# Cosine through an integer conversion read from PSUM, and float64 weights converted 1024 wide

## The chip, the cores and the metric

The kernel runs on one core of a Trainium2 chip. The metric is the device time of one execution in microseconds (us). Each kernel is run several times, and the median counts.

## The reference

Three layers follow one another on 4608 tokens (8 batches of 576) of 512 values:

```python
kv = np.einsum('bhsd,bhse->bhde', k, v)                  # attention without softmax, 8 heads of 64
out = np.einsum('bhsd,bhde->bhse', q, kv)
x = out / np.sqrt(np.mean(out * out, -1, keepdims=True) + 1e-6) * g_norm
h = x @ w_in                                             # 512 -> 2048, w_in and w_out are float64
g = h * np.cos(h)
x = g @ w_out                                            # 2048 -> 512
idx = np.argmax(x @ w_gate, axis=1)                      # one of 8 experts for each token
out[mask] = gate_w[mask, None] * (np.maximum(xe @ w1[e], 0.0) @ w2[e])   # expert e on its tokens
```

The change is in the middle layer: in how `h * cos(h)` is computed, and in how `w_in` and `w_out` are brought from float64 to pairs of float16.

## The kernel before

Every float32 operand is split into two float16 parts, high and low, and a product is three matmuls (high·high, high·low, low·high). TensorE issues them through `mm3`, lines 102 to 104; the profile tells the products apart by their tiles. A split elsewhere is `split` (lines 88 and 89): ScalarE writes the high part, VectorE the low one.

The program is one straight list, written out by hand (`manual_schedule`): each engine works through its own queue in order, and waits where a semaphore is not yet there. Nothing is reordered.

Before the loop stands a prelude (`SEQ0`) with the attention of the first batch and the first two weight tiles of `w_in`. Then come nine blocks of 512 tokens, `b` = 0 to 8, each of 32 half-steps `hs`; `fb = hs // 2` counts the 16 slices of 128 of the 2048 hidden columns. An even half-step issues `g1(b, fb)`: 12 matmuls into the PSUM tile `hps`. An odd one issues `g2(b, fb - 2)`: 12 matmuls that take `gh`, `gl` of the slice two before and the weights `woh`, `wol` into the four tiles `yps`. The last two `g2` of a block are issued at the start of the next. The PSUM tiles `hps` come from a pool of two (`psh`), the tiles `yps` from a pool of four.

Between `g1` and `g2` of a slice lies the cosine. `h` arrives in turns (the weights are scaled by 1 / 2 pi on the way, and by 2 pi in `w_out`). ScalarE copies `hps` to `hs` in SBUF (line 475). VectorE adds a large number so that the sum rounds to whole turns (line 482) and takes it off again, and `hs` as well (line 483); ScalarE takes the absolute value (478) and the sine (479). In `cos_b`, VectorE multiplies by `hs` (496), ScalarE writes `gh` (493), and GpSimd writes `gl` (494).

In block 0 the weights are converted as well, in `conv_w`, a tile of 1 MB in two halves of 512 columns a partition: three VectorE instructions put the float32 bits together (228, 231, 234), ScalarE scales (240) and writes the high half (241), and GpSimd subtracts for the low half (242). One half falls on each half-step up to `hs` = 25, and on 28 and 29; the instructions of ScalarE and GpSimd for a half are issued one half-step later. The tiles come through a ring of four staging tiles; the next load is issued when a tile has been read (`used`).

The rest is side work, put into half-steps by the tables `SEQ1` and `SEQ`: attention of the next block (query splits `nat`, `kvh`/`kvl`, products `ops`, the squares `sq` on GpSimd, their sums `ssq`, the Newton steps of `norm`, lines 422 to 434, the products with `rs` on GpSimd, line 443, then the splits `nat` and the DMA transposes into `xT`, of which `c3` is the last), and the routing of the block before (`r_evac`: four splits from `yps` to `yrow`, at half-step 3). In the last block, `split_x` converts weights of the first expert (`w1h`, `w1l`) ahead of the copy of `hps`, and at half-step 22 `pass_head` casts the counts on VectorE (line 586) and has TensorE add them up (`tps`, line 588). After the blocks come the eight experts, without cosine or conversion.

Of the kernel before, what the change touches and what calls it, by code (L numbers as in the profile page):

```python
# [18 lines left out]
# Float32 operands are split into float16 pairs (hi + lo, scaled by powers of  # L19
# two so that both parts are normal numbers); a product is hi*hi + hi*lo + lo*hi.  # L20
# [5 lines left out]
# Each expert's list has room for all tokens; its first CAP rows are computed  # L26
# for every expert, what lies beyond them only if it is there. The last block
# of tokens goes behind row HEAD, so that the rows before are complete early.
# [7 lines left out]
def tile_attn_moe_moe(ctx: ExitStack, tc: tile.TileContext, q, k, v, g_norm, w_in, w_out, w_gate, w1, w2, out):  # L36
# [17 lines left out]

    const = ctx.enter_context(tc.tile_pool(name="const", bufs=1))
# [7 lines left out]
    # a row: the token (hi, lo), its logits and its number  # L63
# [28 lines left out]
    # Steps of the side work are emitted in two parts, the second (returned) a  # L92
    # little later, so that no engine waits for another's part of the same step.
# [12 lines left out]
    def setup_consts(pre):  # L106
# [10 lines left out]
        # summed over the partitions: the row where the list of each expert starts  # L117
# [13 lines left out]
    # ------------------------------------------------------------------  # L131
    # Phase 1: attention and the dense layer, block by block of 512 tokens
    # ------------------------------------------------------------------
# [3 lines left out]
    gring = ctx.enter_context(tc.tile_pool(name="gring", bufs=LAG + 2))  # L137
    p1 = ExitStack()
# [29 lines left out]
    def load_kv_first():  # L168
        # in parts, in the order of use
        for i in range(2):  # L170
            for nm in "kv":
                load_kv_part(0, nm, 4 * i, 4 * i + 4)
            if i == 0:
                for nm in "kv":
                    load_kv_left(0, nm)
# [20 lines left out]
    # The weights of the dense layer come in float64: its bits are cut to float32 on the chip.  # L196
# [12 lines left out]
    def conv_w(kind, c, i):  # L209
        t = wst[kind, c]  # L210
        if kind == "i":
            src = t[:, :, 128 * i:128 * i + 128]
            o = (c % 4) * 256 + 128 * i
            dh, dl = [w[c // 4].rearrange("p (k f) -> p k f", k=KD)[:, :, o:o + 128] for w in (wih, wil)]
            sc = gs
        else:
            src = t[:, i:i + 1]
            o = (c % 4) * 2 + i
            dh, dl = [w[c // 4].rearrange("p (k f) -> p k f", k=8)[:, o:o + 1] for w in (woh, wol)]
            sc = S_WOUT * TWO_PI  # L220
        sh = list(src.shape)[:3]
        lo, hi = src[:, :, :, 0], src[:, :, :, 1]
        vi = b3.tile(sh, I32, tag="vi", name="vi")
        vf = vi.bitcast(F32)

        def bits(n):
            if n == 0:
                nc.vector.tensor_scalar(out=vi, in0=hi, scalar1=3, scalar2=0x3FFFFFFF, op0=ALU.logical_shift_left,
                                        op1=ALU.bitwise_and)
            elif n == 1:  # L230
                nc.vector.scalar_tensor_tensor(out=vi, in0=hi, scalar=-0x40000000, in1=vi, op0=ALU.bitwise_and,
                                               op1=ALU.bitwise_or)
            else:
                nc.vector.scalar_tensor_tensor(out=vi, in0=lo, scalar=29, in1=vi, op0=ALU.logical_shift_right,
                                               op1=ALU.bitwise_or)
                if i == 1:
                    used()

        def late():
            nc.scalar.activation(out=vf, in_=vf, func=AF.Copy, scale=sc)  # L240
            nc.scalar.activation(out=dh, in_=vf, func=AF.Copy)
            nc.gpsimd.tensor_tensor(out=dl, in0=vf, in1=dh, op=ALU.subtract)  # L242

        return [call(bits, n) for n in range(3)], late

    # Loads run ahead as far as the ring of staging tiles allows.
# [20 lines left out]
    def split_kv(b, nm, j):  # L267
        # a quarter of the tokens (j < 4), or those left over
# [41 lines left out]
    # The first two batches: VectorE is taken by the weights, so k and v go in  # L310
    # as they are; only k is laid out anew.
# [11 lines left out]
    def hot(n):  # L323
        # keeps TensorE at its full clock until the data is there
        ps = psh.tile([128, 512], F32, tag="h", name="hot")
        for _ in range(n):
            nc.tensor.matmul(out=ps[:, 0:128], lhsT=ident, rhs=ident, start=True, stop=True)
# [30 lines left out]
    def split_t(dst, src, scale):  # L358
        # split and turned
# [58 lines left out]
    def norm(b, i):  # L418
        # rs = (mean square + eps) ** -0.5: a bit-level guess and Newton steps
# [47 lines left out]
    # h is kept in turns (h / 2 pi, scaled): cos sees the distance from the nearest whole turn  # L467
    def cos_a(b, fb, ps):
        big = 1.5 * 2.0 ** 23 * S_H
        hs = b3.tile([128, 512], F32, name="hs")  # L470
        u = b3.tile([128, 512], F32, name="u")
        hu[b, fb] = (hs, u)

        def first():
            nc.scalar.activation(out=hs, in_=ps, func=AF.Copy, scale=S_H / (S_X * S_WIN))  # L475

        def late():
            nc.scalar.activation(out=u, in_=u, func=AF.Abs, scale=TWO_PI / S_H)  # L478
            nc.scalar.activation(out=u, in_=u, func=AF.Sin, scale=-1.0, bias=half_pi)  # L479

        return first, [
            lambda: nc.vector.tensor_scalar(out=u, in0=hs, scalar1=big, scalar2=None, op0=ALU.add),  # L482
            lambda: nc.vector.scalar_tensor_tensor(out=u, in0=u, scalar=big, in1=hs, op0=ALU.subtract, op1=ALU.subtract)  # L483
        ], late

    def cos_b(b, fb):
        hs, u = hu.pop((b, fb))
# [8 lines left out]
        return [lambda: nc.vector.tensor_tensor(out=u, in0=hs, in1=u, op=ALU.mult)], late  # L496
# [43 lines left out]
    def choose(b):  # L540
        # first index of the largest logit, and how many earlier tokens chose each expert
# [41 lines left out]
    def totals():  # L583
        # over all partitions: where each expert's next row is
# [37 lines left out]
    # ------------------------------------------------------------------  # L622
    # Phase 2: one expert after the other
    # ------------------------------------------------------------------
# [87 lines left out]
    # ------------------------------------------------------------------  # L712
    # Program
    # ------------------------------------------------------------------
# [7 lines left out]
    # the order in which the staging tiles are used  # L722
# [12 lines left out]
    for e in range(E):  # L735
        for c in range(2):
            add_load(load_w1, e, c, ready=lambda e=e: e == 0 or xs_done)
        for c in range(2):
            add_load(load_w2, e, c, ready=lambda e=e: e == 0 or xs_done)

    # The side work: what comes before the first block, and in which of a block's 32
    # steps the parts for the next block (the second one, those after) are emitted.
    ATT = {"a": attn_a, "b": attn_b, "d": attn_d, "n": attn_n, "m": attn_m, "c": attn_c}
    SEQ0 = ("hot a0 kc0 a1 kv0 kc1 a2 a3 kv1 wi00 b0 b1 d0 d1 b2 b3 kd0 d2 d3 kd1 kd2 kd3 kw0 n0 Wi00 "
            "n1 m0 m1 m2 m3 wi01 c0 c1 c2 c3 Wi01 wi10 wi11 Wi10 Wi11").split()
# [5 lines left out]
    with tc.manual_schedule():  # L751
        pump()
        nc.gpsimd.memset(half_pi, math.pi / 2.0)
# [235 lines left out]
```

## Time and profile before

| | |
|---|---|
| time, median of 3 runs | 1341.68 us (1340.82 to 1343.31) |
| span of the profiled execution | 1342.1 us |
| TensorE busy | 1269.9 us, 95% |
| VectorE busy | 771.8 us, 58% |
| ScalarE busy | 664.8 us, 50% |
| GpSimd busy | 398.4 us, 30% |

A busy TensorE means that a matmul is under way; one matmul is recorded longer (0.38 us for 512 columns) than the distance to the next. The page cuts the span into 40 slices of 33.6 us. In its row for TensorE the first six slices read 6, 8, 7, 7, 6, 8 (tenths), and nearly all later ones 9; in the row for VectorE the second to the fifth read 9. The row of the clock granted to TensorE reads 7 to 9 in the first seven slices and 9 (which stands for 90% and more) after that. So the time in which TensorE is not at work lies in the prelude and block 0, with some in the last block and at the end of the program.

### The profile page before, as it was taken

What the parts mean: (1) busy time and instruction counts of PE and PEld (TensorE: products, weight loads), DVE (VectorE), ACT (ScalarE), POOL (GpSimd) and SP (SyncE); (2) the same over time, 40 slices, a digit from 0 to 9 for tenths busy, and PEclk for the clock granted to TensorE, in tenths of its full rate; (3) what the DMA queues carried; (4) which work ended last, traced back from release to release, by engine and by line L of the source; (5) the groups of instructions that cost most, each with busy time, mean ns of one, the idle gap of its engine ahead of it and who ended that gap; (6) DMA issues with size and microseconds to landing.
All of it is one profiled execution on the core that took longest, in us unless ns stands there. A gap on an engine that the chain in (4) does not pass through costs nothing.

```text
span 1342.1 us, 18677 instructions
## 1 busy us (share of the span) xinstructions
PE 1269.9 (95%) x7236; PEld 661.1 (49%) x7236; DVE 771.8 (58%) x1323; ACT 664.8 (50%) x1178; POOL 398.4 (30%) x386
## 2 busy tenths in 40 slices
PE   6877689999999999999999999989999999999995
PEld 6423235445444554454444444435665665655553
DVE  4999965767767568577574565554543334235211
ACT  3565556565665656656655555444533333334221
POOL 3356622524425335244253352232100100110110
PEclk7889889999999999999999999999999999999998
DMA  8455369353513425144145330034935425525000
GB/s 264 160 134 180 94 177 281 93 115 62 149 42 73 133 56 133 42 64 96 24 64 166 86 73 16 17 108 121 273 116 155 127 90 170 141 95 115 32 21 23
DMA packets 242929, 146.97 MB, mean 110 GB/s; under 512 B 197262, under 2 KB 214670, under 8 KB 242832
## 3 DMA queue, kind: packets, MB, share of 16 engines
q1 hardware_dynamic: 236064, 126.51, 37.6%
q0 software_dynamic: 6080, 19.18, 4.0%
q8 instruction: 58, 0.95, 0.3%
q14 instruction: 39, 0.32, 0.1%
q10 hardware_dynamic: 688, 0.02, 0.0%
HBM read 78.99 MB, written 31.03 MB: 82 GB/s over the span
## 4 chain that ended last, share of the span: by engine, by line
PE 66%; DVE 17%; issue 6%; ACT 6%; DMA 3%; POOL 1%; SPq 0%; POOLq 0%; DVEq 0%; ACTq 0%
PE yps L102 6%; PE hps L102 6%; PE yps L104 6%; PE yps L103 6%; PE hps L103 6%; PE hps L104 6%; PE ops L102 5%; PE ops L104 5%; PE ops L103 5%; PE h1ps L102 4%; PE h1ps L103 4%; PE h1ps L104 4%; DVE u L482 3%; DVE u L483 3%; DVE u L496 2%
## 5 line engine op out<-in xcount | busy, mean ns | idle before, releaser
L494 POOL TENSOR_TENSOR gl<-u,gh 128x512 f16<-128x512 f32 x144 | 173.9, 1208 | 392.3 <-ACT gh L493 330.9
L102 PE MATMUL yps<-woh,gh 128*128 128x512 f16 x576 | 224.3, 389 | 21.0 <-ACT gh L493 14.9
L104 PE MATMUL yps<-woh,gl 128*128 128x512 f16 x576 | 225.5, 391 | 13.1 <-POOL gl L494 12.9
L103 PE MATMUL yps<-wol,gh 128*128 128x512 f16 x576 | 224.4, 390 | 1.6 <-POOL wol L242 1.6
L102 PE MATMUL hps<-xT,wih 128*128 128x512 f16 x576 | 219.0, 380 | 4.4 <-DMA xT<-nat 2.5
L103 PE MATMUL hps<-xT,wih 128*128 128x512 f16 x576 | 218.5, 379 | 0.3 <-DVE xT L89 0.3
L104 PE MATMUL hps<-xT,wil 128*128 128x512 f16 x576 | 218.3, 379 | 0.0
L478 ACT ACTIVATE u<-u 128x512 f32<-128x512 f32 x144 | 90.7, 630 | 252.1 <-DVE u L483 222.2
L482 DVE TENSOR_SCALAR u<-hs 128x512 f32<-128x512 f32 x144 | 120.1, 834 | 112.7 <-ACT hs L475 112.3
L496 DVE TENSOR_TENSOR u<-hs,u 128x512 f32<-128x512 f32 x144 | 102.9, 715 | 124.9 <-ACT u L479 124.8
L697 DVE SCALAR_TENSOR_TENSOR h1l<-h1ps,h1h 128x256 f16<-128x256 f32 (+1 forms) x128 | 62.7, 490 | 184.6 <-ACT h1h L696 180.4
L102 PE MATMUL h1ps<-xeT,w1h 128*128 128x256 f16 (+1 forms) x512 | 153.2, 299 | 0.6 <-DVE h1l L697 0.3
L104 PE MATMUL h1ps<-xeT,w1l 128*128 128x256 f16 (+1 forms) x512 | 153.2, 299 | 0.0
L103 PE MATMUL h1ps<-xeT,w1h 128*128 128x256 f16 (+1 forms) x512 | 153.2, 299 | 0.0
L709 POOL DMA_INDIRECT out_dram<-ob,ei x40 | 39.4, 986 | 356.0 <-ACT ob L708 296.8
L483 DVE SCALAR_TENSOR_TENSOR u<-u,hs 128x512 f32<-128x512 f32 x144 | 121.2, 841 | 5.0
L493 ACT ACTIVATE gh<-u 128x512 f16<-128x512 f32 x144 | 90.6, 629 | 64.1 <-DVE u L496 63.9
L104 PE MATMUL ops<-w2h,h1l 128*128 128x512 f16 x320 | 121.3, 379 | 0.0
L103 PE MATMUL ops<-w2l,h1h 128*128 128x512 f16 x320 | 121.3, 379 | 0.0
L102 PE MATMUL ops<-w2h,h1h 128*128 128x512 f16 x320 | 121.3, 379 | 0.0
L708 ACT ACTIVATE ob<-ops,gt 128x512 f32<-128x512 f32 x40 | 27.5, 688 | 176.8 <-PE ops L104 146.0
L479 ACT ACTIVATE u<-u,half_pi 128x512 f32<-128x512 f32 x144 | 103.9, 722 | 4.7
(154 smaller groups left out, 1892.2 us busy)
## 6 DMA issues: line engine op xcount, KB each, us to landing
w1s<-in_moe_w_dram SPq DMA_DIRECT2D x16, 1024.0 KB, 4.8
w2s<-in_moe_w_dram SPq DMA_DIRECT2D x16, 1024.0 KB, 5.5
xs<-pre SPq DMA_DIRECT2D x8, 1320.0 KB, 7.3
wst<-in_moe_w_in_dram SPq DMA_DIRECT2D x8, 1024.0 KB, 5.8
wst<-in_moe_w_out_dram SPq DMA_DIRECT2D x8, 1024.0 KB, 4.8
kst<-in_k_dram SPq DMA_DIRECT2D x7, 1024.0 KB, 8.7
vst<-in_v_dram SPq DMA_DIRECT2D x7, 1024.0 KB, 6.8
qst<-in_q_dram SPq DMA_DIRECT2D x28, 256.0 KB, 4.7
```

The costliest lines, as they stand in the source:

```text
L102: nc.tensor.matmul(out=o, lhsT=ah, rhs=bh, start=first, stop=False)
L103: nc.tensor.matmul(out=o, lhsT=ah, rhs=bl, start=False, stop=False)
L104: nc.tensor.matmul(out=o, lhsT=al, rhs=bh, start=False, stop=last)
L478: nc.scalar.activation(out=u, in_=u, func=AF.Abs, scale=TWO_PI / S_H)
L479: nc.scalar.activation(out=u, in_=u, func=AF.Sin, scale=-1.0, bias=half_pi)
L482: lambda: nc.vector.tensor_scalar(out=u, in0=hs, scalar1=big, scalar2=None, op0=ALU.add),
L483: lambda: nc.vector.scalar_tensor_tensor(out=u, in0=u, scalar=big, in1=hs, op0=ALU.subtract, op1=ALU.subtract)
L493: nc.scalar.activation(out=gh, in_=u, func=AF.Copy)
L494: nc.gpsimd.tensor_tensor(out=gl, in0=u, in1=gh, op=ALU.subtract)
L496: return [lambda: nc.vector.tensor_tensor(out=u, in0=hs, in1=u, op=ALU.mult)], late
L697: nc.vector.scalar_tensor_tensor(out=dl, in0=ps, scalar=0.0, in1=dh, op0=ALU.max, op1=ALU.subtract)
L709: nc.gpsimd.indirect_dma_start(out=out, out_offset=bass.IndirectOffsetOnAxis(ap=eid[e, i], axis=0), in_=ob, in_offset=None, bounds_check=N ...
```

## The change

Cosine: ScalarE writes `n`, an int32 tile, straight from `hps`, as h plus a quarter turn, rounded by the conversion. VectorE then computes h − n in one instruction that reads `hps` in PSUM. The range is moved by the quarter turn so that ScalarE's sine takes h − n with a positive scale and the bias, without an absolute value. The product with h reads `hps` a second time. So `hps` is held until `cos_b`, and `hs` is gone.

Weights: `conv_w` works on the whole tile, 1024 columns. It has three parts: `bits` (three VectorE instructions), `high` (one ScalarE instruction with the scale in it), `low` (one VectorE instruction in place of ScalarE's scaling and GpSimd's subtraction). They are issued at half-steps `hs`, `hs + 1` and `hs + 2`. The comments are taken out; line numbers shift.

```diff
-    def conv_w(kind, c, i):
-        t = wst[kind, c]
+    def conv_w(kind, c):
+        t = wst.pop((kind, c))
...
-        vi = b3.tile(sh, I32, tag="vi", name="vi")
+        vi = vip.tile(sh, I32, tag="vi", name="vi")
...
-        def late():
-            nc.scalar.activation(out=vf, in_=vf, func=AF.Copy, scale=sc)
-            nc.scalar.activation(out=dh, in_=vf, func=AF.Copy)
-            nc.gpsimd.tensor_tensor(out=dl, in0=vf, in1=dh, op=ALU.subtract)
+        def high():
+            nc.scalar.activation(out=dh, in_=vf, func=AF.Copy, scale=sc)
+
+        def low():
+            nc.vector.scalar_tensor_tensor(out=dl, in0=vf, scalar=sc, in1=dh, op0=ALU.mult, op1=ALU.subtract)
+
+        return [bits, high, low]
...
         def first():
-            nc.scalar.activation(out=hs, in_=ps, func=AF.Copy, scale=S_H / (S_X * S_WIN))
+            nc.scalar.activation(out=n, in_=ps, func=AF.Copy, scale=1.0 / (S_X * S_WIN), bias=0.25)
 
         def late():
-            nc.scalar.activation(out=u, in_=u, func=AF.Abs, scale=TWO_PI / S_H)
-            nc.scalar.activation(out=u, in_=u, func=AF.Sin, scale=-1.0, bias=half_pi)
+            nc.scalar.activation(out=u, in_=u, func=AF.Sin, scale=SIN_SCALE, bias=half_pi)
 
         return first, [
-            lambda: nc.vector.tensor_scalar(out=u, in0=hs, scalar1=big, scalar2=None, op0=ALU.add),
-            lambda: nc.vector.scalar_tensor_tensor(out=u, in0=u, scalar=big, in1=hs, op0=ALU.subtract, op1=ALU.subtract)
+            lambda: nc.vector.scalar_tensor_tensor(out=u, in0=ps, scalar=1.0 / (S_X * S_WIN), in1=n, op0=ALU.mult,
+                                                   op1=ALU.subtract)
         ], late
...
-        return [lambda: nc.vector.tensor_tensor(out=u, in0=hs, in1=u, op=ALU.mult)], late
+        return [lambda: nc.vector.scalar_tensor_tensor(out=u, in0=ps, scalar=S_H / (S_X * S_WIN), in1=u, op0=ALU.mult,
+                                                       op1=ALU.mult)], late
...
-                if b == 0 and hs % 4 < 2:
-                    ops, wlate = conv_w("o", hs // 4, hs % 2)
-                elif b == 0 and hs < 26:
-                    ops, wlate = conv_w("i", hs // 4 + 2, hs % 2)
+                if b == 0 and hs % 4 == 0 or 0 == b and hs % 4 == 2 and hs < 26:
+                    conv[hs] = conv_w(*(("o", hs // 4) if hs % 4 == 0 else ("i", hs // 4 + 2)))
+                ops = [conv[h].pop(0) for h in (hs - 2, hs) if conv.get(h)]
+                wprev = conv[hs - 1].pop(0) if conv.get(hs - 1) else None
```

VectorE's queue in block 0, one slice (`fb` = 3, a tile of `w_in`), before; `vi` is the tile of bits, `wst` the staged float64:

```order
L228 TENSOR_SCALAR vi<-wst 128x512
L231 SCALAR_TENSOR_TENSOR vi<-wst,vi 128x512
L234 SCALAR_TENSOR_TENSOR vi<-wst,vi 128x512
L482 TENSOR_SCALAR u<-hs 128x512
L483 SCALAR_TENSOR_TENSOR u<-u,hs 128x512
L228 TENSOR_SCALAR vi<-wst 128x512
L231 SCALAR_TENSOR_TENSOR vi<-wst,vi 128x512
L234 SCALAR_TENSOR_TENSOR vi<-wst,vi 128x512
L496 TENSOR_TENSOR u<-hs,u 128x512
```

The same slice on VectorE now:

```order
L242 SCALAR_TENSOR_TENSOR wol_141<-vi,woh_140 128x1024
L230 TENSOR_SCALAR vi<-wst 128x1024
L232 SCALAR_TENSOR_TENSOR vi<-wst,vi 128x1024
L234 SCALAR_TENSOR_TENSOR vi<-wst,vi 128x1024
L481 SCALAR_TENSOR_TENSOR u<-hps,n 128x512
L495 SCALAR_TENSOR_TENSOR u<-hps,u 128x512
```

The low half of the tile before stands first, and the two cosine instructions now follow each other with nothing between them.

ScalarE's queue at the same place, from the copy of one `hps` to the next `gh`, before:

```order
L475 ACTIVATE hs<-hps 128x512
L240 ACTIVATE vi<-vi 128x512
L241 ACTIVATE woh_137<-vi 128x512
L478 ACTIVATE u<-u 128x512
L479 ACTIVATE u<-u,half_pi 128x512
L88 ACTIVATE wgp<-wg 128x4x8
L240 ACTIVATE vi<-vi,gs 128x512
L241 ACTIVATE wih_133<-vi 128x4x128
L493 ACTIVATE gh<-u 128x512
```

and now:

```order
L475 ACTIVATE n<-hps 128x512
L478 ACTIVATE u<-u,half_pi 128x512
L90 ACTIVATE wgp<-wg 128x4x8
L239 ACTIVATE wih_136<-vi,gs 128x4x256
L492 ACTIVATE gh<-u 128x512
```

The one wide conversion stands behind the sine and ahead of `gh`; VectorE's low half of the same tile is the instruction after the second cosine instruction.

TensorE's queue holds the same instructions in the same order. On SyncE's queue one load of `w_out` now stands ahead of two of the four `qT` transposes of block 0. GpSimd's queue loses the 32 subtractions of line 242.

## Rows read from the trace of the kernel before

**Rows 1.** Busy time by stage: us, then PE, PEld, DVE, ACT, POOL, clock, DMA.
```profile
40.00:173.00 133.00, 100.19 (x427) 42.14 (x426) 129.75 (x163) 78.48 (x135) 72.52 (x52) 0.88 0.47 137
...
200.00:700.00 500.00, 498.06 (x2953) 246.58 (x2951) 338.13 (x591) 298.83 (x510) 191.56 (x175) 1.00 0.41 95
700.00:880.00 180.00, 173.19 (x938) 79.63 (x937) 103.35 (x172) 93.39 (x156) 61.85 (x61) 1.00 0.30 71
```

**Rows 2.** TensorE's waits: for whom, us in total, times, longest.
```profile
PE yps L102 <- ACT gh L493: 14.9, 7, 6.3
...
PE tps L588 <- DVE acc L586: 3.7, 1, 3.7
...
PE yps L102 <- DVE yrow L89: 2.7, 2, 1.4
PE hps L102 <- DMA xT<-nat: 2.5, 1, 2.5
```

**Rows 3.** VectorE's timeline in block 0: start, duration (us), instruction.
```profile
48.07 0.41 DVE L482 TENSOR_SCALAR u<-hs 128x512 f32<-128x512 f32 x1
...
90.20 0.42 DVE L228 TENSOR_SCALAR vi<-wst 128x512 int32<-128x512 int32 x1
90.65 0.69 DVE L231 SCALAR_TENSOR_TENSOR vi<-wst,vi 128x512 int32<-128x512 int32 x1
...
93.77 1.53 DVE L234 SCALAR_TENSOR_TENSOR vi<-wst,vi 128x512 int32<-128x512 int32 x1
...
151.80 0.42 DVE L482 TENSOR_SCALAR u<-hs 128x512 f32<-128x512 f32 x1
...
169.62 0.68 DVE L89 SCALAR_TENSOR_TENSOR nat<-x,nat 128x512 f16<-128x512 f32 x1
```

**Rows 4.** GpSimd's timeline, the subtraction beside the fourth of Rows 3.
```profile
94.72 1.59 POOL L494 TENSOR_TENSOR gl<-u,gh 128x512 f16<-128x512 f32 x1
```

**Rows 5.** Timeline of the prelude: a VectorE pair that reads PSUM, beside GpSimd.
```profile
30.37 1.16 POOL L242 TENSOR_TENSOR wil<-vi,wih 128x512 f16<-128x512 f32 x1 [19.51 <-ACT wih L241]
30.46 1.29 DVE L440 SCALAR_TENSOR_TENSOR x<-ops,rs 128x512 f32<-128x512 f32 x2
```

**Rows 6.** Groups by form, experts' stage: busy us, mean ns, idle before.
```profile
L696 ACT ACTIVATE h1h<-h1ps 128x384 f16<-128x384 f32 x64 | 31.4, 491 | 66.0 <-PE h1ps L104 66.0
...
L696 ACT ACTIVATE h1h<-h1ps 128x256 f16<-128x256 f32 x64 | 24.5, 383 | 28.7 <-PE h1ps L104 28.2
```

**Rows 7.** The same view for VectorE.
```profile
L697 DVE SCALAR_TENSOR_TENSOR h1l<-h1ps,h1h 128x384 f16<-128x384 f32 x64 | 35.6, 557 | 53.3 <-ACT h1h L696 53.3
L697 DVE SCALAR_TENSOR_TENSOR h1l<-h1ps,h1h 128x256 f16<-128x256 f32 x64 | 27.1, 423 | 131.3 <-ACT h1h L696 127.1
```

**Rows 8.** ScalarE's timeline at the start of block 1.
```profile
179.52 0.58 ACT L475 ACTIVATE hs<-hps 128x512 f32<-128x512 f32 x1
...
184.14 0.63 ACT L493 ACTIVATE gh<-u 128x512 f16<-128x512 f32 x1 [0.76 <-DVE u L496]
184.68 0.58 ACT L475 ACTIVATE hs<-hps 128x512 f32<-128x512 f32 x1
...
187.82 0.72 ACT L479 ACTIVATE u<-u,half_pi 128x512 f32<-128x512 f32 x1
188.45 2.04 ACT L88 ACTIVATE yrow<-yps 128x512 f16<-128x512 f32 x4
```

**Rows 9.** TensorE's timeline at the start of block 1.
```profile
190.04 0.59 PE L102 MATMUL yps<-woh,gh 128*128 128x512 f16 x1 [3.33 <-ACT yrow L88]
...
195.11 0.63 PE L102 MATMUL hps<-xT,wih 128*128 128x512 f16 x1
```

**Rows 10.** TensorE's timeline in the last block, behind the wait for the counts.
```profile
877.69 0.38 PE L102 MATMUL yps<-woh,gh 128*128 128x512 f16 x1
877.91 0.38 PE L103 MATMUL yps<-wol,gh 128*128 128x512 f16 x1
...
881.92 0.42 PE L102 MATMUL hps<-xT,wih 128*128 128x512 f16 x1
```

## What is predicted, and why

> **What bounds the kernel now.** I read the busy time by stage first. From 200 to 700 us TensorE is busy 498.06 of 500 us at full clock: nothing that other engines save there can shorten the run [rows 1]. Between 40 and 173 us (block 0) it is busy only 100.19 of 133 us, at a mean granted clock of 0.88, while VectorE is busy 129.75 us: VectorE's queue bounds that stage. Between 700 and 880 us TensorE loses another 6.8 us. TensorE's waits say on whom: 14.9 us on `gh`, 3.7 us on the counts in the last block, 2.7 us on the low parts of `yrow`, 2.5 us on the last transposes into `xT` at the start of block 1 [rows 2].
>
> Why VectorE is full shows in its timeline. An instruction on two SBUF tensors takes 0.69 us alone (90.65) and 1.53 us at 93.77; GpSimd's subtraction, recorded from 94.72 for 1.59 us, overlaps its end [rows 3, 4]. The VectorE instruction ends at 95.30, and GpSimd then needs 1.01 us until 96.31, about what it takes alone: the two take turns. Against that, two VectorE instructions that read PSUM and one SBUF tensor begin at 30.46, 0.09 us after a GpSimd subtraction; the pair takes 1.29 us, and the subtraction 1.16 us: neither waits [rows 5].
>
> **The change part by part.** Widths first. VectorE goes from 423 to 557 ns for 128 more columns [rows 7], so 512 more cost 0.54 us, and a two-tensor instruction of 1024 takes 1.23 us (start to start 1.26 when the next needs its result, 1.14 when not). The first instruction of `bits` takes 0.42 us at 512 [rows 3]; with the same fixed part of 0.15 us it is 0.69 at 1024. ScalarE goes from 383 to 491 ns [rows 6], so its wide copy takes 0.63 [rows 8] plus 0.43, 1.06 us. For `n`, an int32 result, there is no row: between 0.58 us, the copy it replaces, and 0.72 us, the sine; I take 0.58, since only the output type differs.
>
> The two cosine instructions read PSUM and one SBUF tensor. I price them at 0.69 us, and at nothing for GpSimd [rows 5]. [...]
>
> One slice in block 0, from the start of its first cosine instruction: 0.72 until the sine starts, 0.63 until ScalarE's next can start (187.82 to 188.45 [rows 8]), 1.06 for `high`, which stands behind the sine, 0.03 for the semaphore. VectorE has meanwhile done the second cosine instruction and waits, because `low` needs `high`: it starts at 2.44. `gh` is written at about 3.0; `gl` then stands behind `low` until 3.67, runs to 4.68, and the first of `bits` ends 0.55 later, at 5.23. The other two take 0.03 + 1.26 + 1.14. The next slice's cosine starts at 7.66 us.
>
> [...]
>
> Side work: eight small ScalarE copies fall between sine and `high` over slices 0 to 12, 5 at about 0.5, 2 at 0.38, 1 at 0.15, together 3.4 us. VectorE's own side work mostly fits into its wait, except about 0.9 us of the Newton steps. GpSimd's squares also fall into waits. Start: the last split of the prelude ends at 40.07; the second tile's `bits`, `high`, `low` and the third tile's `bits` in sequence give 48.74 for the first cosine, 0.67 later than 48.07 now [rows 3]. So slice 12 starts at 48.74 + 12 × 7.66 + 3.4 + 0.9 = 144.96, against 151.80.
>
> From there to the end of the attention chain: Newton steps 1.3, two products on GpSimd and two splits alternating with them, then `high` and `low`, 7.5 us to slice 13; 6.2 to slice 14 (one tile's `bits`, with GpSimd in between); 0.7 + 0.6 for the last split, 3.3 for its transpose (170.30, the end of the split at 169.62, to 173.60, TensorE's first matmul of block 1). That is 18.3 us, against 21.8 now. TensorE starts block 1 at 163.3 instead of 173.6: **10.2 us gained**.
>
> Start of block 1. Before, ScalarE's queue is a ring: each copy of `hps` stands behind `gh` of the slice before, 5.16 us a round (179.52 to 184.68 [rows 8]), as long as the 24 matmuls of a slice (24 × 0.215 [rows 10]). So it never catches up, `yrow` starts at 188.45, though its matmuls were done at 184.1 (190.04 less the wait of 3.33 and one `g1` of 2.58 [rows 9]), and TensorE waits 3.33 us and then runs at half clock: 12 matmuls take 5.07 us instead of 2.58 [rows 9]. The new ring is 0.58 + 0.69 + 0.72 + 0.69 + 0.63 less overlaps, 3.2 us, and `yrow` follows its matmuls directly. Gain 3.33 + 2.49 = 5.8 us. But TensorE waits 2 us for `xT` at the end of block 0, and I charge 1.7 us for a half-clock stretch behind it, the like of what the last block shows: 4.23 us instead of 2.58 [rows 10]. **Net 4.1 us.**
>
> Last two blocks: the same shorter ring ends the two waits on `yrow` (2.7 us). In the last block a weight split stands in the ring: 0.6 us on ScalarE and 0.7 on VectorE more, 4.5 us in all, less than the 5.16 of a slice, where the old ring with it was longer. So the counts come in time: 3.7 less 0.2 us, and the half clock behind them, 1.65 us. **7.8 us.** Smaller waits are left out.
>
> At no cost: `hps` is held longer, but in full-speed blocks its second reader ends 2.8 us after `g1` (0.58 + 0.69 + 0.72 + 0.69 and semaphores), and the third slice needs the tile 7.7 us after. If side work of over 4.9 us got into that chain, TensorE would wait for the rest. The load of `w_out` moved ahead of two transposes delays them by one load; their reader is five half-steps away, 19 us. The experts' stage has no changed instruction.
>
> Sum: 10.2 + 4.1 + 7.8 = 22.1 us from the profiled 1342.1, which is 0.4 above the median of the runs: 1319.6. I take 1319.
>
> **The rivals.** (a) Block 0 gets no shorter: `low` behind `high` behind the sine is a new wait, and if `gl` hits the later `bits` too, or `n` takes much longer, a slice costs 0.8 us more and the 10.2 are gone; the other gains stay: 1330. For it: VectorE idles some 0.3 us or more in each slice, which it does not now. (b) `gl` gets in before `low` and lands in that wait: a slice costs about 0.9 less, 12 us: 1308. [...] (d) PSUM-reading instructions beside GpSimd are no quicker in bulk than in the one pair shown, and the ring stays near a slice's length: most of block 1's and the last block's gain goes, and with block 0's the run is within 0.2%: 1341.
>
> **How the numbers follow.** Forecast 1319: 0.45 (its own range 1312 to 1326). (a) 0.25, (b) 0.17, (c) 0.08, (d) 0.05. A measurement of this kernel can tell about 0.2% (2.7 us) from no change. The range 1304 to 1333 takes in the forecast, (a) and most of (b). Faster 0.87, same 0.05, slower 0.08.
>
> **What would show it.** A slice in block 0 from one first cosine instruction to the next at 7.5 to 7.9 us without side work, VectorE's gap ahead of `low` ended by `high`; the two cosine instructions at 0.69 us even beside GpSimd; block 1's first matmul near 163 us; no wait on `yrow` and none over 0.5 us on the counts; 200 to 700 us unchanged. It is wrong if TensorE waits for `hps` tiles in the full blocks, or if the clock in block 0 falls under 0.8.

## The result, and the profile after

| | before | after |
|---|---|---|
| time, median | 1341.74 us (1340.82 to 1343.31) | 1318.20 us (1317.32 to 1320.76) |
| span of the profiled execution | 1342.1 us | 1319.1 us |
| TensorE busy | 1269.9 us | 1260.3 us |
| VectorE busy | 771.8 us | 629.5 us |
| ScalarE busy | 664.8 us | 559.6 us |
| GpSimd busy | 398.4 us | 342.7 us |

The ratio is 0.9826, with a 95% interval of 0.9812 to 0.9840. A second measurement of the changed kernel (e10 below) gave 1317.69 us and a ratio of 0.9819 (0.9804 to 0.9834).

Where the 23.0 us between the two spans lie is read from TensorE's timeline, at the first matmul of `g1` in a block. All the kernels of this document are in one table (the labels are those of the experiments below):

| kernel | first `g1` of block 0 to that of block 1 | block 1 | blocks 2 to 8 | behind them |
|---|---|---|---|---|
| before | 134.12 us | 101.44 | 630.24 | 436.8 |
| after | 126.25 | 94.85 | 621.99 | 436.6 |
| after, the second measurement (e10) | 126.17 | 93.46 | 621.98 | 435.9 |
| e1, cosine alone | 121.94 | 94.13 | 621.98 | 436.4 |
| e2, weights alone | 144.21 | 97.60 | 630.04 | 436.5 |
| e3, low between | 113.31 | 93.90 | 621.98 | 436.3 |
| e4, no `gl` in block 0 | 114.78 | 93.60 | 621.98 | 436.3 |
| e5, both | 103.64 | 93.71 | 621.99 | 436.0 |
| e6, e3 in halves | 122.09 | 93.25 | 621.98 | 435.6 |
| e7, e3 with `gl` on VectorE | 110.32 | 93.88 | 621.99 | 436.5 |
| e8, wide, low on GpSimd | 119.17 | 93.94 | 621.98 | 436.5 |
| e9, e7 with the first low later | 108.84 | 92.98 | 621.99 | 436.3 |

So the change gained 7.9 us in block 0, 6.6 in block 1 and 8.2 in the blocks behind. The first `g1` itself stands between 37.1 and 39.5 us in these executions, whatever the kernel, so distances are compared and not clock readings.

Busy time of the profile after, by stage, with the columns and stretches of [rows 1]:

```profile
40.00:173.00 133.00, 102.71 (x454) 45.24 (x454) 111.56 (x122) 51.73 (x81) 34.75 (x24) 0.91 0.56 155
200.00:700.00 500.00, 500.00 (x2918) 246.62 (x2917) 253.37 (x498) 248.64 (x422) 189.33 (x185) 1.00 0.43 97
700.00:880.00 180.00, 179.07 (x971) 82.81 (x970) 77.56 (x143) 79.49 (x129) 57.24 (x57) 1.00 0.26 64
```

The stretches are those of before by the clock; in its work the changed kernel is 8 us further on at 173 us, and 23 at 880. The full-speed blocks have no gap left: 500.00 of 500 us, where 1.94 were missing. Their VectorE time fell by 85 us and their ScalarE time by 50, and that was worth no more than those 1.94 us. In the first line VectorE is still the busiest, now with gaps.

TensorE's waits after (from 38 us on), against [rows 2]:

```profile
PE hps L104 <- DVE u L495: 26.1, 12, 5.7
PE hps L104 <- DMA xT<-nat: 3.0, 1, 3.0
PE tps L588 <- DVE acc L586: 0.9, 1, 0.9
...
PE yps L106 <- POOL gl L493: 0.6, 1, 0.6
```

One large wait of before stands neither in [rows 2] nor in the prediction's list of TensorE's waits. It is the second largest, and lies in block 0:

```profile
PE yps L104 <- POOL gl L494: 12.9, 11, 2.2
```

It fell to 0.6 us. The waits on `gh` (14.9) and on `yrow` (2.7, and the 3.33 of [rows 9]) are gone. A new one stands in their place: `hps` is released by the second cosine instruction (line 495), so TensorE's waits in block 0 now go by that name. It is the same cause, VectorE's queue.

One slice of block 0 on VectorE after (start, duration, instruction, and in brackets the wait ahead of it), to be read beside [rows 3]:

```profile
89.12 0.68 DVE L481 SCALAR_TENSOR_TENSOR u<-hps,n 128x512 f32<-128x512 f32 x1
90.59 0.69 DVE L495 SCALAR_TENSOR_TENSOR u<-hps,u 128x512 f32<-128x512 f32 x1 [0.79 <-ACT u L478]
91.63 1.28 DVE L242 SCALAR_TENSOR_TENSOR wil<-vi,gs,wih 128x1024 f16<-128x1024 f32 x1 [0.35 <-ACT wih L239]
92.83 1.64 DVE L230 TENSOR_SCALAR vi<-wst 128x1024 int32<-128x1024 int32 x1
94.51 1.23 DVE L232 SCALAR_TENSOR_TENSOR vi<-wst,vi 128x1024 int32<-128x1024 int32 x1
95.77 1.23 DVE L234 SCALAR_TENSOR_TENSOR vi<-wst,vi 128x1024 int32<-128x1024 int32 x1
96.92 0.68 DVE L481 SCALAR_TENSOR_TENSOR u<-hps,n 128x512 f32<-128x512 f32 x1
```

GpSimd's only work beside it, to be read beside [rows 4]:

```profile
92.25 1.68 POOL L493 TENSOR_TENSOR gl<-u,gh 128x512 f16<-128x512 f32 x1 [6.11 <-ACT gh L492]
```

The slice takes 7.80 us and has three stops: 0.79 us for the sine, 0.35 for `high`, and 0.96 in the first instruction of `bits`, which takes 1.64 us here and 0.68 where GpSimd is idle. `gl` is recorded from 0.62 us into `low` on; both it (1.68 us, against the 1.16 of a subtraction alone) and `bits` pay for the encounter.

VectorE's groups over the first twelve slices (count, busy us, mean ns, idle ahead of them) are what the experiments are compared by:

```profile
L230 DVE TENSOR_SCALAR vi<-wst 128x1024 int32<-128x1024 int32 x12 | 18.8, 1565 | 0.0
L234 DVE SCALAR_TENSOR_TENSOR vi<-wst,vi 128x1024 int32<-128x1024 int32 x13 | 15.9, 1225 | 0.4
L232 DVE SCALAR_TENSOR_TENSOR vi<-wst,vi 128x1024 int32<-128x1024 int32 x12 | 15.4, 1285 | 0.4
L495 DVE SCALAR_TENSOR_TENSOR u<-hps,u 128x512 f32<-128x512 f32 x12 | 8.3, 690 | 7.7 <-ACT u L478 7.7
L481 DVE SCALAR_TENSOR_TENSOR u<-hps,n 128x512 f32<-128x512 f32 x12 | 8.2, 684 | 0.0
L242 DVE SCALAR_TENSOR_TENSOR wil<-vi,gs,wih 128x1024 f16<-128x1024 f32 x6 | 7.7, 1282 | 1.9 <-ACT wih L239 1.9
L242 DVE SCALAR_TENSOR_TENSOR wol<-vi,woh 128x1024 f16<-128x1024 f32 x6 | 7.4, 1236 | 1.1 <-ACT woh L239 0.8
```

`bits` 50.1 us (one instruction of line 234 that begins before slice 0 is counted in), `low` 15.1, cosine 16.5, waits for ScalarE 10.7: together 92.4, of some 97.8 us from slice 0 to slice 12.

### The profile page after: what moved, and what is told of

It is laid out like the page before. It is cut to its first block, busy times and chain, and to the rows that moved or that the text cites. A ratio compares the mean times of both kernels' runs of the same rounds, so it can differ in the third digit from the quotient of the medians.

```text
span 1319.1 us, 18338 instructions
## 1 busy us (share of the span) xinstructions
PE 1260.3 (96%) x7236; PEld 660.3 (50%) x7236; DVE 629.5 (48%) x1147; ACT 559.6 (42%) x986; POOL 342.7 (26%) x354
## 4 chain that ended last, share of the span: by engine, by line
PE 81%; DVE 7%; issue 4%; DMA 4%; ACT 2%; POOL 0%; SPq 0%; POOLq 0%; ACTq 0%; DVEq 0%
PE yps L104 8%; PE yps L105 8%; PE yps L106 8%; PE hps L104 8%; PE hps L106 8%; PE hps L105 8%; PE ops L104 5%; PE ops L105 5%; PE ops L106 5%; PE h1ps L104 4%; PE h1ps L105 4%; PE h1ps L106 4%; DVE vi L230 1%; DVE vi L232 1%; DMA out_dram<-ob,ei 1%
## 5 line engine op out<-in xcount | busy, mean ns | idle before, releaser
L104 PE MATMUL hps<-xT,wih 128*128 128x512 f16 x576 | 223.1, 387 | 29.9 <-DVE u L495 26.1
L481 DVE SCALAR_TENSOR_TENSOR u<-hps,n 128x512 f32<-128x512 f32 x144 | 99.4, 690 | 270.7 <-ACT n L475 270.6
L105 PE MATMUL hps<-xT,wih 128*128 128x512 f16 x576 | 222.2, 386 | 0.7 <-DVE xT L91 0.7
L106 PE MATMUL hps<-xT,wil 128*128 128x512 f16 x576 | 222.6, 386 | 0.0
L106 PE MATMUL yps<-woh,gl 128*128 128x512 f16 x576 | 218.3, 379 | 0.7 <-POOL gl L493 0.6
L104 PE MATMUL yps<-woh,gh 128*128 128x512 f16 x576 | 218.5, 379 | 0.0
L105 PE MATMUL yps<-wol,gh 128*128 128x512 f16 x576 | 218.4, 379 | 0.0
L475 ACT ACTIVATE n<-hps 128x512 int32<-128x512 f32 x144 | 85.6, 595 | 187.8 <-PE hps L106 183.4
L495 DVE SCALAR_TENSOR_TENSOR u<-hps,u 128x512 f32<-128x512 f32 x144 | 99.2, 689 | 60.6 <-ACT u L478 59.8
L105 PEld LDWEIGHTS <-wih 128*128 128x128 f16 x576 | 57.2, 99 | 92.1 <-issue 34.4
```

The source lines that it names most:

```text
L104: nc.tensor.matmul(out=o, lhsT=ah, rhs=bh, start=first, stop=False)
L105: nc.tensor.matmul(out=o, lhsT=ah, rhs=bl, start=False, stop=False)
L106: nc.tensor.matmul(out=o, lhsT=al, rhs=bh, start=False, stop=last)
L475: nc.scalar.activation(out=n, in_=ps, func=AF.Copy, scale=1.0 / (S_X * S_WIN), bias=0.25)
L481: lambda: nc.vector.scalar_tensor_tensor(out=u, in0=ps, scalar=1.0 / (S_X * S_WIN), in1=n, op0=ALU.mult, op1=ALU.subtract)
L495: return [lambda: nc.vector.scalar_tensor_tensor(out=u, in0=ps, scalar=S_H / (S_X * S_WIN), in1=u, op0=ALU.mult, op1=ALU.mult)], late
```

## The experiments

The theory: VectorE's queue bounds block 0, and what counts there is its own instructions, the stops in its order, and GpSimd's turns; behind block 0 only the shorter cosine ring counts. The first rival: the wide conversions carry the gain. The second: PSUM-reading instructions are no quicker beside GpSimd in bulk (rival (d) of the prediction).

**e1, the cosine alone.** The kernel before with the new `cos_a` and `cos_b`; the weights are converted as before.

```diff
-            nc.scalar.activation(out=hs, in_=ps, func=AF.Copy, scale=S_H / (S_X * S_WIN))
+            nc.scalar.activation(out=n, in_=ps, func=AF.Copy, scale=1.0 / (S_X * S_WIN), bias=0.25)
...
-        return [lambda: nc.vector.tensor_tensor(out=u, in0=hs, in1=u, op=ALU.mult)], late
+        return [lambda: nc.vector.scalar_tensor_tensor(out=u, in0=ps, scalar=S_H / (S_X * S_WIN), in1=u, op0=ALU.mult,
+                                                       op1=ALU.mult)], late
```

> The kernel before with the new cosine alone; the weights are converted in halves of 512 columns with ScalarE's scaling and GpSimd's subtraction, as before. My theory: a slice of block 0 costs VectorE 2 x 1.78 us for the bits, 2 x 0.60 for the cosine and three turns given up to GpSimd at 0.85, 7.3 us, against 7.9 before, since the first cosine instruction of 0.45 us is gone; the two that read PSUM stay at 0.69 us beside GpSimd's three subtractions a slice. The shorter ring of ScalarE and VectorE brings all of what it brought at the start of block 1, on yrow and on the counts. Sum: 6.6 + 4 + 8 to 9 us, 1322 us. The rival, that each part brings about half: 1330 us. A third, that reading PSUM beside GpSimd is not free in bulk: the two instructions at 1.2 us or more where a subtraction runs, and 1335 us or more.

Measured: 1314.45 us (1313.79 to 1315.04), ratio 0.9796 (0.9779 to 0.9812). The size was missed by 7.5 us, and the order of the two kernels was wrong: half of the change is 3.2 to 3.8 us faster than the whole. VectorE's groups over the same twelve slices, first of before, then of this kernel:

```profile
L234 DVE SCALAR_TENSOR_TENSOR vi<-wst,vi 128x512 int32<-128x512 int32 x25 | 27.3, 1093 | 0.9
L231 DVE SCALAR_TENSOR_TENSOR vi<-wst,vi 128x512 int32<-128x512 int32 x24 | 22.6, 941 | 0.8
L482 DVE TENSOR_SCALAR u<-hs 128x512 f32<-128x512 f32 x12 | 13.5, 1124 | 0.0
L483 DVE SCALAR_TENSOR_TENSOR u<-u,hs 128x512 f32<-128x512 f32 x12 | 12.5, 1039 | 0.4
L228 DVE TENSOR_SCALAR vi<-wst 128x512 int32<-128x512 int32 x24 | 11.5, 478 | 0.0
L496 DVE TENSOR_TENSOR u<-hs,u 128x512 f32<-128x512 f32 x12 | 10.0, 833 | 0.0
```

```profile
L235 DVE SCALAR_TENSOR_TENSOR vi<-wst,vi 128x512 int32<-128x512 int32 x25 | 30.6, 1225 | 0.9
L232 DVE SCALAR_TENSOR_TENSOR vi<-wst,vi 128x512 int32<-128x512 int32 x24 | 25.8, 1077 | 0.8
L229 DVE TENSOR_SCALAR vi<-wst 128x512 int32<-128x512 int32 x24 | 15.9, 661 | 0.0
L495 DVE SCALAR_TENSOR_TENSOR u<-hps,u 128x512 f32<-128x512 f32 x12 | 8.2, 681 | 0.0
L481 DVE SCALAR_TENSOR_TENSOR u<-hps,n 128x512 f32<-128x512 f32 x12 | 8.1, 678 | 0.0
```

The cosine fell from 36.0 to 16.3 us. Some 5 us of that are the instruction that is gone (12 of 0.41 us); the rest are turns, since all three instructions had met GpSimd's turns, 16 times in the 36 (1.26 to 1.64 us each, where the others took 0.41 to 0.69), and none of the two new ones does (0.68 us on average). `bits` took over some of the turns, 61.4 to 72.3 us. Net 8.8 us; the twelve slices went from 103.7 to 94.2 us. VectorE has no stop at the sine (the idle time ahead of line 495 is 0.0): between the two cosine instructions stand three of `bits`, in whose time the sine is done. The whole change needs 92.4 us for the same list, against 88.6 here: its conversions and low halves take 65.2 us instead of 72.3, but its stops cost 10.7.

**e2, the weights alone.** The changed kernel with the cosine of before; the diff is that of e1 turned round.

> The changed kernel with the cosine of before; the weights are converted 1024 wide, the low half on VectorE. My theory: low waits for high, which stands behind the absolute value and the sine; from the first cosine instruction 0.45 + 0.72 + 0.65 + 0.63 + 1.06 + 0.03 us until low can start, then low, a turn for gl and the bits, 8.7 us a slice, more than the 7.9 before. Block 0 gets longer by some 8 to 10 us, and nothing of the rest comes: 1350 us, slower than before. The rival, that the width and the removed subtractions on GpSimd make block 0 shorter by themselves (32 turns of 0.85 us fewer): 1334 us or less.

Measured: 1347.49 us (1346.15 to 1348.74), ratio 1.0045 (1.0029 to 1.0062): slower than before. VectorE's timeline at the sine of this kernel:

```profile
94.00 0.69 DVE L484 SCALAR_TENSOR_TENSOR u<-u,hs 128x512 f32<-128x512 f32 x1
96.20 0.69 DVE L497 TENSOR_TENSOR u<-hs,u 128x512 f32<-128x512 f32 x1 [1.51 <-ACT u L480]
97.24 1.28 DVE L242 SCALAR_TENSOR_TENSOR wil<-vi,gs,wih 128x1024 f16<-128x1024 f32 x1 [0.35 <-ACT wih L239]
```

The stop at the sine is 1.51 us, against 0.79 in the slice of the change above, since the absolute value (0.63 us in the kernel before) stands ahead of it, and block 0 is 10.1 us longer than before. The last blocks (630.04 against 630.24 us) have all their old waits: there the ring's gain is the cosine's alone. Not so in block 1, where something came that was not expected: it is 3.8 us shorter than before (97.60 against 101.44), with the old ring. TensorE waits there longer for the transposes,

```profile
PE hps L104 <- DMA xT<-nat: 3.8, 1, 3.8
```

and its granted clock is 0.66 in the 5 us behind that wait. So ScalarE's first copy of block 1 starts 0.2 us behind its `g1`, where it started 3.3 us behind in the kernel before (179.52 against 173.60 + 2.58), and the wait of 3.33 us on `yrow` is not there. A shorter ring is one way to end that wait; TensorE's later and slower start is another.

**e3, low between.** The changed kernel with `low` issued between the two cosine instructions instead of behind them; it now stands behind the `bits` of the next tile and not ahead of them.

```diff
-                ops = [conv[h].pop(0) for h in (hs - 2, hs) if conv.get(h)]
+                ops = [conv[hs].pop(0)] if conv.get(hs) else []
+                low = [conv[hs - 2].pop(0)] if conv.get(hs - 2) else []
...
-                for f in cos:
+                for f in cos + low:
                     f()
```

> The changed kernel with low moved: it is issued between the two cosine instructions of its half-step instead of ahead of the bits, so it fills VectorE's wait for the sine, and high was done a whole slice before. My theory, that VectorE's queue with its wait bounds block 0: a slice takes 0.60 + 1.14 + 0.60 + 0.72 + 1.26 + 1.14 + 0.9 = 6.4 us instead of 7.7, block 1 starts 12 to 15 us earlier, and the run takes 1305 us. The rival, that TensorE's wait for a free hps tile (26.1 us in the changed kernel) is a bound of its own: block 0 gets little shorter, 1315 us or more.

Measured: 1305.01 us (1304.67 to 1306.30), ratio 0.9727 (0.9711 to 0.9743). No work was taken away, only VectorE's stops. The start of one slice in VectorE's timeline:

```profile
86.84 0.68 DVE L481 SCALAR_TENSOR_TENSOR u<-hps,n 128x512 f32<-128x512 f32 x1
87.44 1.27 DVE L242 SCALAR_TENSOR_TENSOR wil<-vi,gs,wih 128x1024 f16<-128x1024 f32 x1
88.64 0.68 DVE L495 SCALAR_TENSOR_TENSOR u<-hps,u 128x512 f32<-128x512 f32 x1
89.24 0.67 DVE L91 SCALAR_TENSOR_TENSOR nat<-qst,nat 128x512 f16<-128x512 f32 x1
89.84 0.68 DVE L230 TENSOR_SCALAR vi<-wst 128x1024 int32<-128x1024 int32 x1
90.55 2.08 DVE L232 SCALAR_TENSOR_TENSOR vi<-wst,vi 128x1024 int32<-128x1024 int32 x1
```

`low` fills the time of the sine, and its `high` is done long before. What is left of the stop at the sine, over twelve slices, is that of the first slice, which has no `low` to put there:

```profile
L495 DVE SCALAR_TENSOR_TENSOR u<-hps,u 128x512 f32<-128x512 f32 x12 | 8.2, 680 | 0.8 <-ACT u L478 0.8
```

The slices' mean goes from 8.15 to 6.92 us (47.50 to 130.57 over 12), 1.23 less. The stops were 1.14 us in the slice shown above and 0.89 on average (10.7 over twelve), and 0.07 of that is left. The rest is in smaller parts: `bits` loses 0.16 us a slice, one `low` of the twelve (0.10 a slice) now falls behind the stretch, and instructions with no stop ahead of the next one overlap with it by some 0.1 us. GpSimd's turn is still there, now in the second of `bits` (2.08 us instead of 1.22) or in the third.

**e4, no `gl` in block 0.** The changed kernel without line 493 in block 0; the low half of `g` is left out for the first 512 tokens, and a tile of zeros stands in its place.

```diff
-            nc.gpsimd.tensor_tensor(out=gl, in0=u, in1=gh, op=ALU.subtract)
+            if b:
+                nc.gpsimd.tensor_tensor(out=gl, in0=u, in1=gh, op=ALU.subtract)
```

> The changed kernel without GpSimd's subtraction in block 0: the low half of g is zero there, for the first 512 tokens. My theory: each subtraction costs VectorE 0.95 us, always in the first of the bits, so a slice takes 6.7 us instead of 7.7 and the run 1306 us. The rival, that the turn is not on the path (VectorE waits for high anyway): 7.7 us a slice, 1318 us.

Measured: 1305.45 us (1305.36 to 1305.59), ratio 0.9727 (0.9711 to 0.9744). A slice takes 7.18 us on average instead of 8.15, 0.97 less (0.95 expected). In VectorE's timeline the stops stay and the turn is gone:

```profile
77.46 0.69 DVE L498 SCALAR_TENSOR_TENSOR u<-hps,u 128x512 f32<-128x512 f32 x1 [0.79 <-ACT u L480]
...
80.06 0.69 DVE L232 TENSOR_SCALAR vi<-wst 128x1024 int32<-128x1024 int32 x1
```

**e5, both.** The edits of e3 and e4 together.

> The third and the fourth kernel's edits together: low between the two cosine instructions, and no gl in block 0 (the low half of g is left out for the first 512 tokens, so this is a bound and no kernel to use). Theory (the wait of VectorE for sine and high, 1.14 us a slice, and GpSimd's turn, about 0.9 us a slice, are two separate costs): a slice of block 0 goes from 6.92 us (low between alone) to about 6.0, still over the 5.6 us that TensorE takes for a slice in the later blocks, so the run gains 11 to 13 us more: 1293 us (1291 to 1297). Rival (both edits remove the same idle time, whichever is made first): 1304 to 1306 us, as each alone.

Measured: 1294.03 us (1292.80 to 1294.32), ratio 0.9639 (0.9623 to 0.9655). Together the edits take off 22.6 us from block 0 (126.25 to 103.64), alone 12.9 and 11.5, so only 1.8 us of the sum are lost: the stops and the turn are two separate costs, and VectorE's queue bounds block 0 nearly down to here.

**e6, e3 in halves.** The same order as e3, but each instruction of `bits`, `high` and `low` issued as two of 512 columns.

```diff
-            nc.scalar.activation(out=dh, in_=vf, func=AF.Copy, scale=sc)
+            for _, f, _, _, h, _ in cuts:
+                nc.scalar.activation(out=h, in_=f, func=AF.Copy, scale=sc)
...
```

> Low between the two cosine instructions, in the same order, but each conversion instruction of 1024 columns is issued as two of 512. Theory (the width saves the fixed part of the three bits instructions, 0.18 us each): start to start three of 512 take 0.45 + 0.72 + 0.66 us, two sets 3.66 instead of 3.12, so 0.54 us a slice, 6.5 us over 12 slices: 1311 us. Rival (finer instructions let GpSimd and the cosine in earlier, and the width is worth nothing): 1303 to 1306 us.

Measured: 1313.69 us (1312.07 to 1315.24), ratio 0.9792 (0.9776 to 0.9809). A slice takes 7.52 us (48.30 to 138.48 over 12) instead of 6.92: the width of `bits` and `low` together is worth 0.60 us a slice (0.54 expected from `bits` alone), another 0.9 us ahead of the first slice, and 8.7 us between the two medians, in an order without stops.

**e7, `gl` of block 0 on VectorE.** e3, with `gl` of block 0 behind the first of `bits`, on VectorE.

```diff
-            nc.gpsimd.tensor_tensor(out=gl, in0=u, in1=gh, op=ALU.subtract)
+            if b:
+                nc.gpsimd.tensor_tensor(out=gl, in0=u, in1=gh, op=ALU.subtract)
+            else:
+                gpend.append(lambda: nc.vector.tensor_tensor(out=gl, in0=u, in1=gh, op=ALU.subtract))
...
```

> Low between the two cosine instructions, and gl of block 0 computed on VectorE, behind the first bits instruction of the next half-step, instead of on GpSimd. Theory (a turn of GpSimd costs VectorE about 0.85 us a slice, the instruction itself 0.6): 0.25 us a slice, 3 us: 1302 us. Rival (VectorE now waits for gh, which ScalarE writes behind high and the copies of the queries): 1305 us or more. Where VectorE is not the only bound any more, gain under 2 us.

Measured: 1302.72 us (1301.28 to 1303.57), ratio 0.9703 (0.9687 to 0.9719). On VectorE the subtraction takes 0.69 us and 0.6 from start to start, less than the turn it replaces (2.06 to 2.08 us instead of 1.22 in e3). The gain on e3 is small, 2.3 us between the medians, and the intervals of the two ratios overlap; the two sets of times don't meet, and block 0 is 3.0 us shorter in the trace (110.32 against 113.31), as expected.

**e8, wide, with the low halves on GpSimd.** The changed kernel, with ScalarE scaling in place and GpSimd subtracting, as before, but 1024 wide.

```diff
-            nc.scalar.activation(out=dh, in_=vf, func=AF.Copy, scale=sc)
-
-        def low():
-            nc.vector.scalar_tensor_tensor(out=dl, in0=vf, scalar=sc, in1=dh, op0=ALU.mult, op1=ALU.subtract)
-
-        return [bits, high, low]
+            nc.scalar.activation(out=vf, in_=vf, func=AF.Copy, scale=sc)
+            nc.scalar.activation(out=dh, in_=vf, func=AF.Copy)
+            nc.gpsimd.tensor_tensor(out=dl, in0=vf, in1=dh, op=ALU.subtract)
+
+        return [bits, high]
...
```

> The full change with its 1024-wide conversions, but the low halves stay as they were: ScalarE scales in place and copies, GpSimd subtracts, 1024 wide. Beside the cosine-alone run (1314.45 us) only the width differs; beside the full change (1318.2) only where the low halves are made. Theory (the move of low onto VectorE, into a place where it waits, is what costs): no wait of VectorE for high, two turns of GpSimd a slice of which the wide one costs VectorE up to 1.8 us, 0.54 us of fixed parts saved against cosine alone: 1310 us (1306 to 1315). Rival (the width is what costs, since a wide instruction holds up what stands behind it): 1318 us or more.

Measured: 1310.34 us (1309.84 to 1311.48), ratio 0.9765 (0.9748 to 0.9781). So the width helps here too: e8 is 4.1 us under e1, although its two cosine instructions stand side by side, so that VectorE stops for the sine (8.0 us in the twelve slices) where e1 doesn't. And it is the move of `low` onto VectorE, into a place where VectorE has to stop for it, that costs 7 to 8 us: 5.5 in the twelve slices (92.3 us from 44.42 on, against 97.8), and 2.5 ahead of them (from the first `g1` to the first cosine instruction 7.15 us, against 9.66). In the twelve slices the move brings 15.1 us of `low` and 3.0 of stops ahead of it, and takes only 12.7 us of turns out of `bits`. The turn is longer and still cheaper than the move. VectorE's third `bits` instruction, and GpSimd's two subtractions beside it:

```profile
85.54 3.03 DVE L234 SCALAR_TENSOR_TENSOR vi<-wst,vi 128x1024 int32<-128x1024 int32 x1
```

```profile
85.13 2.36 POOL L241 TENSOR_TENSOR wil<-vi,wih 128x1024 f16<-128x1024 f32 x1 [2.61 <-ACT wih L240]
87.45 2.14 POOL L492 TENSOR_TENSOR gl<-u,gh 128x512 f16<-128x512 f32 x1
```

**e9, the first low later.** e7, with the low half of the second tile of `w_in` moved from the prelude to between the first slice's two cosine instructions.

```diff
...
-            "n1 m0 m1 m2 m3 yi0 c0 c1 c2 c3 wi1 xi1 yi1").split()
+            "n1 m0 m1 m2 m3 yi0 c0 c1 c2 c3 wi1 xi1").split()
...
+                if b == 0 and hs == 0:
+                    low = [conv0]
```

> The seventh kernel (low between, gl of block 0 on VectorE), and the low half of the second tile, for which VectorE waits 1.22 us ahead of the first slice, moved between the first slice's two cosine instructions, where VectorE waits 0.79 us for the sine. Theory (VectorE's queue is the only bound of block 0, so each idle us ahead of it counts in full): 1.2 + 0.8 = 2.0 us less, 1300.7 us. Rival (TensorE, which starts the third slice only when that low half and the PSUM tile are there, loses it again): 1302.7 us or more.

Measured: 1299.90 us (1299.22 to 1300.66), ratio 0.9686 (0.9673 to 0.9699). That is 2.8 us under e7, where 2.0 were expected: in the traces block 0 is 1.5 us shorter and block 1 0.9. The rival has a part in it: the first cosine instruction comes 2.2 us earlier (7.12 us behind the first `g1` instead of 9.33), but the third slice takes 8.26 us instead of 6.99, since VectorE waits 1.12 us there for `kvh`, which waits for TensorE's products `kvps`. This is the fastest of the kernels that compute everything, 18 us under the change itself.

**e10, the full change again.**

> The full change once more, beside the kernel before on this chip, so that the other kernels' ratios can be set against it: 1318 us (1316 to 1321), a ratio of 0.982 to 0.983. If it came out at 1315 or less, what the weights part costs on top of the cosine alone would be chip to chip variation.

Measured: 1317.69 us (1317.14 to 1318.59). The intervals of its ratio and of e1's overlap a little (from 0.9804 to 0.9812), but the eight times of the full change (1317.14 to 1320.76) and the four of e1 (1313.79 to 1315.04) don't meet, and block 0 is 4.2 us longer in the trace (126.17 against 121.94). So the weights part does cost some 3 to 4 us on top of the cosine alone, as the groups above say.

## Why the prediction was right, and which terms were off

The time, 1318.2 us, is the forecast's (1319, range 1304 to 1333), by the mechanism it named: VectorE's queue gave back time in block 0, and the waits behind it ended, in the last blocks by the shorter ring. The terms were less exact than their sum: block 0 was put 2.3 us too high and block 1 2.5 us too low, and that the two cancel is luck.

**Block 0: 10.2 us predicted (its own 173.6 − 163.3 is 10.3), 7.9 measured.** The slice itself was right: 7.66 us predicted, 7.64 and 7.80 where ScalarE has no side copy. Its stops came as predicted. The turn for `gl` hit the first of `bits`, in eleven of the twelve slices (the twelfth has none in `bits`); one square on GpSimd hit the second, once (1.94 us). The mis-sized term is the side work over slices 0 to 12, 4.3 us predicted (3.4 + 0.9); 97.82 − 12 × 7.66 leaves 5.9 us. Of the 1.6 us between, some 0.7 are not side work: the slices in which `high` and `low` work on a tile of `w_in` take 7.8 us. The start (49.06 us instead of 48.74) and the end (18.77 instead of 18.3 us) add 0.3 and 0.5.

**Start of block 1: 4.1 us predicted, 6.6 measured.** ScalarE's timeline after, beside [rows 8]:

```profile
175.37 0.60 ACT L475 ACTIVATE n<-hps 128x512 int32<-128x512 f32 x1 [2.00 <-PE hps L106]
176.79 0.72 ACT L478 ACTIVATE u<-u,half_pi 128x512 f32<-128x512 f32 x1 [0.83 <-DVE u L481]
177.42 2.04 ACT L90 ACTIVATE yrow<-yps 128x512 f16<-128x512 f32 x4
179.32 0.65 ACT L492 ACTIVATE gh<-u 128x512 f16<-128x512 f32 x1
```

The ring has slack now: ScalarE waits 2.00 us for TensorE, where TensorE waited for ScalarE, and the wait on `yrow` is gone. The 5.8 us are all gained: the wait and the half clock behind it (0.50 from 190.0 to 195.2 us before) are gone. That the shorter ring is enough to end them, e1 shows, where TensorE waits only 0.7 us for `xT` and has its full clock behind it (1.00 from 165 to 180 us). In the changed kernel itself TensorE also waits 3.0 us for `xT`, with the half clock behind it, and behind 3.8 us of the same the old ring was in time as well (e2), so how much of the 5.8 us is the ring's there is open. Left out were two waits on the products of k and v (`kvps`), which are gone after. They stand so among TensorE's waits of before from 173 to 275 us:

```profile
PE kvps L103 <- DVE ks L89: 1.5, 2, 1.1
```

Some 0.7 us of block 1's gain belong to no wait named here.

The half clock behind the wait for `xT` came in the profiled execution as charged, but not in the second measurement's. TensorE's clock (third column from the right; 0.66 is a mean: it reads 1.00 from 165.5 to 166.9 us and 0.50 from 167.0 to 169.9) in the 5 us from 165.5 us on, first after, then e10:

```profile
165.50:170.50 5.00, 4.85 (x15) 1.89 (x16) 0.59 (x1) 1.23 (x2) 1.15 (x1) 0.66 1.29 247
```

```profile
165.50:170.50 5.00, 4.98 (x24) 2.29 (x25) 1.15 (x2) 1.94 (x3) 1.16 (x1) 1.00 1.28 251
```

The waits ahead of the two were 3.02 and 3.03 us. Block 1 took 94.85 us with the fall and 93.46 without it, so the charge of 1.7 us is 1.4 where it falls due.

**Last blocks: 7.8 us predicted, 8.2 measured.** Both waits on `yrow` are gone. The counts were predicted to come 0.2 us late and came 0.9, against the 0.5 that the prediction had set itself; the clock stays at full speed behind that wait (granted clock 1.00 in the 5 us from 856.5 us on). By these terms 7.1 us are gained; some 1.1 of the 8.2 belong to no wait named here.

**The rivals.** (a) needed a slower `n` or a turn in the later `bits`: `n` takes 594 ns on average, and line 234 1225 ns, as alone. (b) needed `gl` ahead of `low`: it starts 0.62 us after. (c), a slower run because the granted clock falls in block 0, did not come: its mean from 40 to 173 us was 0.91, against the 0.88 of [rows 1]. (d) is answered by VectorE's groups after, from 40 to 680 us:

```profile
L481 DVE SCALAR_TENSOR_TENSOR u<-hps,n 128x512 f32<-128x512 f32 x106 | 73.1, 690 | 193.2 <-ACT n L475 193.2
L495 DVE SCALAR_TENSOR_TENSOR u<-hps,u 128x512 f32<-128x512 f32 x106 | 73.0, 688 | 38.2 <-ACT u L478 38.2
```

Set against GpSimd's timeline, instruction by instruction, 27 of the 88 first cosine instructions of 180 to 680 us overlap one of its subtractions, squares or products, 17 of them for over 0.1 us; the mean of the 27 is 0.691 us, and that of the others too. In e1, whose GpSimd is busy for 62 of the 110 us from 40 to 150, 12 of the 27 cosine instructions of that stretch overlap for over 0.1 us, and their mean is 0.680 us. On SBUF the like takes 0.69 us (90.65 in [rows 3]), so a PSUM source costs no more in any of these rows.

**What the prediction did not see** is that its two parts pull against each other. It costed the change against before, part by part, and found `low`'s wait (its rival (a) turns on it), but never costed the cosine alone. Without the conversions the change gives 1314 us (e1), and with the low halves left on GpSimd 1310 (e8).

## What to carry to other kernels

Where one engine's queue bounds a stage, look for the places where it stops for another engine, and put work there whose inputs are long done: here that was worth 13 us, more than half of the whole change's gain, without removing an instruction. Moving work onto that engine paid here only where it doesn't stop for it: `low` cost 7 to 8 us in the one place (after against e8) and gained 5 in the other (e3 against e8). And cost the parts of a change also one by one: a part that loses can hide in a sum that is right.

## What the runs showed of the hardware beyond what was expected

VectorE and GpSimd took turns also at 1024 columns, in the instructions of `bits`; the cosine instructions that read PSUM did not (0.680 us on average in e1, 0.691 in the changed kernel, with GpSimd at work beside them). In e8 VectorE's third `bits` instruction, 1.22 us elsewhere, is recorded with 3.03: it began 0.41 us into a GpSimd subtraction of 2.36, and ended 1.08 us behind it. The next subtraction, of 1.16 us where it is alone, then took 2.14, and ended 1.02 us behind that instruction. Who paid differed with the order of the instructions: in the changed kernel it was the first of `bits` in eleven of twelve slices (1.64 or 1.65 us, against 0.68 alone), in e3 the second or the third (2.06 to 2.08 us, against 1.22).

TensorE's granted clock behind a wait of the same length (3.02 and 3.03 us), at the same place of the same program, fell in one execution (0.66) and not in the other (1.00). What decides it is not shown by these runs.
